# Token scores of the first batch from the state scores, turned by VectorE, in a mixed attention kernel on one core

## The chip, the cores and the metric

The program runs on one core of one Trainium2 chip. Its time is the device time of one execution in microseconds (us), and of several executions the median counts. The engines have queues of their own, in order: TensorE (matmuls), VectorE, ScalarE, GpSimd, and SyncE, which issues the DMAs. A step of one engine waits for steps of another by semaphores.

## The reference

```python
scale = 1.0 / np.sqrt(D)                       # B, H, S, Ns, D = 8, 8, 512, 32, 64
scores = scale * x @ state.T                   # per batch and head: tokens by states
xread = softmax(scores) @ state                # every token reads the state
sread = softmax(scale * state @ x.T) @ x       # every state reads the tokens
x = concat([xread, sread], axis=2)             # 544 tokens of 512 = H * D
logits = x @ w_gate                            # 4 experts, the best 2 of each token
for e in range(4):
    q, k, v = x @ wq[e], x @ wk[e], x @ wv[e]  # 64 wide
    ye = causal_softmax(q @ k.T / 8) @ v @ wo[e]
    out += weight_of_e_for_each_token * ye
```

Both softmaxes of the first part are of the same products x . state: along the states for the tokens, along the tokens for the states.

## The kernel before

Numbers are kept as pairs of 16-bit parts, a high and a low one (`hi_lo` out of PSUM, `split` out of SBUF: one instruction each for the high and the low part), and a product takes three matmuls. A batch goes through four streams. `front` loads x (`xn`), makes the pairs (`xh`), turns them (`xT`), computes the token weights (`eb`, then turned and split into `at`), the state times the weights (`gs`), and from `at` and `gs` the keys `kt`, the values `v`, the gate and the masked queries `qm`. `main` (`probs`, `reads`) does the causal attention in four blocks of 128 tokens. `side` lets the states read the tokens, `tail` does the attention of the 32 state tokens for two batches at once.

The token weights come in one of two ways. Batches from 1 on (`b >= CFG["PA"]`, line 654) call `state_scores`: 24 matmuls of 512 columns give the scores states by tokens in two banks `sa`, from which the state softmax starts (maximum `m2`, exponential `e2`) and which VectorE turns into `eb` (two turns for each half u); the softmax over states follows, VectorE turns the result into `et`, and `split` makes `at`. Batch 0 has 96 small matmuls instead, which give the scores tokens by states in two banks; the softmax reads them there, TensorE turns the weights (4 matmuls for each half, then `hi_lo`), and `side` calls `state_scores` itself.

All steps are numbered as the program makes them, and `run` (line 331) issues them in the written list `ORDER`: number, a dot, and which of a step's possible engines takes it; a third number is a count of fillers, 128-column matmuls on zeros put before the step on TensorE and written to its bank. `SLOTS` gives for each buffer the slot it takes. Both lists come from an offline planner; on the chip each engine follows its own part in order. A warm run of 36 filler matmuls is a step of its own (number 0). The weights of the experts are loaded once in the start-up, in two parts each, into the staging tiles `p32` (384 and 128 KB); `gs` of batch 0 reads them there as they came.

Of the kernel before, what the change touches and what calls it, by code (L numbers as in the profile page):

```python
# [17 lines left out]
           SIDE=32, PX=1, PA=1, LB=1, xn=2, ROUNDS=12, CLIMBS=100, PAT={'PE': 0.15, 'DVE': 0.05},  # L18
# [107 lines left out]
    "mb": "01010101",  # L126
    "p32": "01201222012012010210210201021021021021021",
    "sbm": "01010101",
    "m2": "01010101",
    "s2": "01010101",  # L130
    "kt": "01201020",
    "lg": "010101010101",
# [987 lines left out]
```

## Time and profile before

| | |
|---|---|
| median of three runs | 297.08 us (296.47 to 297.46) |
| the profiled execution's own time | 299.29 us |
| its span in the trace | 297.5 us |
| mean granted TensorE clock | 0.994 of full |
| TensorE matmuls busy | 282.1 us, 95%, 3588 of them |
| VectorE busy | 254.9 us, 86% |
| ScalarE busy | 219.9 us, 74% |
| GpSimd busy | 213.4 us, 72% |

Busy times are shares of the span. Matmuls overlap in their pipeline, so TensorE's busy time includes overlap, and fillers count as busy. Nearly all operations are recorded by one helper (line 347), so they are told apart by the tiles that they write and read, not by their lines.

### The profile page before, as it was taken

What the parts mean: (1) busy time and instruction counts of PE and PEld (TensorE: products, weight loads), DVE (VectorE), ACT (ScalarE), POOL (GpSimd) and SP (SyncE); (2) the same over time, 40 slices, a digit from 0 to 9 for tenths busy, and PEclk for the clock granted to TensorE, in tenths of its full rate; (3) what the DMA queues carried; (4) which work ended last, traced back from release to release, by engine and by line L of the source; (5) the groups of instructions that cost most, each with busy time, mean ns of one, the idle gap of its engine ahead of it and who ended that gap; (6) DMA issues with size and microseconds to landing.
All of it is one profiled execution on the core that took longest, in us unless ns stands there. A gap on an engine that the chain in (4) does not pass through costs nothing. (4 is left out here: it accounts for less than half of the span.)

```text
span 297.5 us, 9631 instructions
## 1 busy us (share of the span) xinstructions
PE 282.1 (95%) x3588; PEld 189.5 (64%) x3588; DVE 254.9 (86%) x783; ACT 219.9 (74%) x677; POOL 213.4 (72%) x293
## 2 busy tenths in 40 slices
PE   8799978898999999999999999999999999999994
PEld 7596565466756565677755586575666667576762
DVE  3877979999999999999999999979998877798640
ACT  4577579889699887977899989646768666647732
POOL 7362787599889797699999995488977942883300
PEclk9979999999999999999999999999999999999999
DMA  7925875998877989999979999988127554385963
GB/s 217 263 47 108 212 121 104 155 236 156 168 158 163 202 176 269 153 173 221 225 152 225 192 155 173 205 184 165 74 65 115 133 97 113 66 156 92 211 197 114
DMA packets 132382, 47.69 MB, mean 160 GB/s; under 512 B 119408, under 2 KB 127856, under 8 KB 132336
## 3 DMA queue, kind: packets, MB, share of 16 engines
q1 hardware_dynamic: 132336, 47.08, 76.9%
q8 instruction: 28, 0.46, 0.7%
q14 instruction: 18, 0.15, 0.2%
HBM read 11.02 MB, written 8.91 MB: 67 GB/s over the span
## 5 line engine op out<-in xcount | busy, mean ns | idle before, releaser
L347 PE MATMUL bank<-kt,qm 128*128 128x128 f16 (+7 forms) x384 | 46.7, 299 | 1.5 <-DVE gs L347 0.7
L347 PE MATMUL bank<-wo_n,z 128*128 128x512 f16 (+1 forms) x198 | 45.8, 373 | 0.1
L347 PE MATMUL bank<-v,pt 128*128 128x192 f16 x480 | 44.8, 246 | 0.9 <-ACT mt L347 0.9
L347 PE MATMUL bank<-at,gs 128*128 128x512 f16 x192 | 45.4, 379 | 0.1
L347 PEld LDWEIGHTS <-pt 128*128 128x128 f16 x480 | 40.4, 98 | 5.8 <-issue 2.3
L347 POOL TENSOR_TENSOR ph<-p,ph 128x256 f16<-128x256 f32 (+3 forms) x22 | 30.8, 1400 | 11.6 <-DVE ph L347 4.3
L347 PEld LDWEIGHTS <-qm 128*128 128x128 f16 (+1 forms) x384 | 23.4, 96 | 22.2 <-issue 8.7
L347 ACT ACTIVATE p<-bank,mx 128x384 f32<-128x384 f32 (+3 forms) x64 | 33.2, 523 | 3.2 <-DVE mx L347 2.3
L347 PEld LDWEIGHTS <-z 128*128 128x128 f16 x198 | 18.5, 98 | 19.5 <-issue 0.8
L347 DVE CUSTOM_DVE_ANT_0 bank<-bank,causal 128x128 f32<-128x128 f32 (+3 forms) x64 | 30.1, 505 | 0.9 <-PE bank L347 0.6
L347 PEld LDWEIGHTS <-gs 128*128 128x128 f16 x192 | 18.1, 99 | 19.6 <-issue 1.3
L347 POOL TENSOR_TENSOR qm<-qf,qm 128x512 f16<-128x512 f32 x21 | 25.9, 1242 | 4.6 <-ACT qm L347 3.9
L347 ACT ACTIVATE o<-bank 128x512 f32<-128x512 f32 (+1 forms) x35 | 19.9, 581 | 7.3 <-PE bank L347 6.7
L347 PE MATMUL bank<-gs,at 128*128 128x260 f16 x192 | 23.6, 273 | 1.1 <-DVE bd L347 0.4
L347 DVE TENSOR_TENSOR qf<-bank,mt 128x512 f32<-128x512 f32 (+1 forms) x32 | 21.3, 683 | 2.4 <-ACT mt L347 2.1
L347 PEld LDWEIGHTS <-at 128*128 128x128 f16 x192 | 18.3, 97 | 6.1 <-issue 1.7
L347 ACT ACTIVATE xh<-xn 128x512 f16<-128x512 f32 (+1 forms) x34 | 19.5, 599 | 3.4 <-DMA xn<-in_x_dram 3.4
L347 POOL TENSOR_TENSOR z<-z 128x128 f32<-128x128 f32 x25 | 12.9, 522 | 10.8 <-DVE z L347 5.4
L345 PE MATMUL bank<-zeros 128*128 128x128 bf16 x236 | 18.1, 247 | 1.4 <-DVE zeros L383 1.0
L347 DVE SCALAR_TENSOR_TENSOR xh<-xn,xh 128x512 f16<-128x512 f32 (+1 forms) x24 | 16.3, 701 | 3.6 <-ACT xh L347 3.2
L345 PEld LDWEIGHTS <-zeros 128*128 128x128 bf16 x236 | 17.1, 114 | 2.6 <-issue 1.6
L347 DVE TENSOR_TENSOR z<-bank,c 128x384 f32<-128x384 f32 x32 | 17.4, 543 | 1.5 <-POOL ph L347 0.9
(193 smaller groups left out, 688.1 us busy)
## 6 DMA issues: line engine op xcount, KB each, us to landing
out_dram<-o SPq DMA_DIRECT2D x33, 256.0 KB, 2.6
xn<-in_x_dram SPq DMA_DIRECT2D x15, 512.0 KB, 4.9
xn<-in_x_dram SPq DMA_DIRECT2D x2, 256.0 KB, 4.1
sn<-in_state_dram SPq DMA_DIRECT2D x16, 32.0 KB, 3.9
p<-in_moe_wo_dram SPq DMA_DIRECT2D x2, 256.0 KB, 5.1
pt<-ph SPq DMA_TRANSPOSE x32, 3.9
z<-zh SPq DMA_TRANSPOSE x29, 2.8
xT<-xh SPq DMA_TRANSPOSE x28, 3.4
```

Source lines behind the costliest of these rows:

```text
L345: self.nc.tensor.matmul(out=to[:, :128], lhsT=self.zeros, rhs=self.zeros, start=True, stop=True, skip_group_check=True)
L347: f(**{k: v.ap() if isinstance(v, View) else v for k, v in kw.items()})
```

## The change

`PA` goes from 1 to 0. Batch 0 then takes the branch of all other batches: `front` calls `state_scores` for it, VectorE turns the scores and the weights, `split` makes `at`, and `side` finds `e2` done. The subtraction of the maximum, which reads SBUF now, may go to GpSimd. `marks["A"]` is not set any more, so the planner is not told to keep the weight splits behind it.

The steps get other numbers: up to 93 they keep theirs; 94 is now the state scores' matmuls; 95 to 100 the state maxima, shifts and exponentials; 101 to 112 the half u=0 (two turns, maximum, subtraction, exponential, sum, plus, reciprocal, product, turn, high part, low part) and 113 to 124 the half u=1; the old 116 to 212 are now 125 to 221, and from the old 220 on all are 2 higher. The list has 2033 steps instead of 2031, and is new throughout, as are the slots. The 130, 125 and 135 of the new list are the matmuls of `gs` with `wk`, `wq` and `wv`; 177 is the first projection. The loads 89 and 90 are of `wk`, 87 and 88 of `wq`, 91 and 92 of `wv`, 318 and 319 of the next batch's x.

```diff
 CFG = dict(ZL=3, GP=1, PT=4, WARM=36, HV=0, BL=1, LEAN0={'DVE': 0.3, 'ACT': 0.0, 'POOL': 0.0}, ZM=4, SM=4, QM=4,
-           SIDE=32, PX=1, PA=1, LB=1, xn=2, ROUNDS=12, CLIMBS=100, PAT={'PE': 0.15, 'DVE': 0.05},
+           SIDE=32, PX=1, PA=0, LB=1, xn=2, ROUNDS=12, CLIMBS=100, PAT={'PE': 0.15, 'DVE': 0.05},
 ORDER = """
...
-5.0 19.0 20.0 21.0 22.0 23.0.41 24.1 4.0 3.0 31.0 1.0 14.0 2.0 8.0 9.0 12.0 26.0 11.0 25.0 32.0 15.0 13.0 27.0 33.0.17 10.0 34.1 35.1 16.0 18.0 17.1
...
+5.0 19.0 20.0 21.0 4.0 3.0 31.0 14.0 12.0 26.0 22.0 2.0 1.0 8.0.48 9.0 32.0 15.0 13.0 27.0 33.0.14 23.0 10.0 24.1 38.0 70.0 45.0 36.0 53.0 41.0 43.0
+81.0 49.0 46.0 39.0 77.0 44.0 54.0 47.0 40.0 51.0 42.0 57.0 82.0 59.0 65.0 72.0 80.0 76.0 71.0 74.0 55.0 75.0 86.0 69.0 58.0 85.0 50.0 66.0 34.1 35.1
+16.0 17.0 18.0 25.0 28.0 29.1 11.0 30.1 94.0.23 113.0 114.0 115.0 0.0 102.0 101.0 103.0 98.0 89.0 202.0 63.0 90.0 205.0 91.0 208.0 7.0 6.0 93.0 214.0
+87.0 92.0 73.0 83.0 37.0 56.0 79.0 61.0 206.1 60.0 116.1 48.0 104.1 88.0 130.0 125.0 135.0 117.0 118.0 119.0 196.0 131.0 105.0 128.0 133.0 95.0 120.0
+121.1 122.0 96.1 126.0 97.0 99.1 123.0 100.0 84.0 198.0 222.0 204.0 207.1 62.0 67.0 68.0 318.0 319.0 106.0 138.0 199.0 326.0 332.0 64.0 124.0 323.0
+320.0 584.0 585.0 590.0.11 329.0 591.0 127.0 107.0 108.0 109.1 327.0 134.0 110.0 129.0 132.0 324.0 328.0 333.1 334.0 111.0 136.0 112.0 211.0 139.0
+592.0 223.0 137.0 325.0 224.0 215.0 330.0 177.0.30 203.0 225.0 178.0 226.0 210.0 78.0 201.1 200.1 197.1 213.1 331.0 227.0 219.0 216.0 588.0 228.0
+229.1 230.0 587.0 586.0 589.0 148.0 321.0 149.0 150.0 151.0 322.0 209.1 174.0 179.0 212.0 144.0 152.0 335.0 175.0 176.0 146.0 147.0 154.0 155.0 336.0
+140.0 145.0 153.0 141.0 337.1 142.0 156.0 220.0 342.0 339.0 157.0 343.0 160.0 158.0 161.0 162.0 354.0 159.0 217.0 338.0 344.0 163.0 340.0 164.0 355.0
...
 SLOTS = {
...
-            st.behind = marks["A"]
+            st.behind = marks.get("A")
```

## Rows read from the trace of the kernel before

**Rows 1.** The table of busy time by stretch. Columns: the stretch, its length, then the busy time and (x instructions) of TensorE's matmuls, its weight loads, VectorE, ScalarE and GpSimd, then the granted clock as a share of full speed, the DMA engines' busy share and GB/s.

```profile
20.00:26.60 6.60, 6.25 (x131) 5.34 (x128) 2.87 (x5) 4.56 (x13) 2.31 (x4) 1.00 0.18 34
26.60:40.00 13.40, 11.91 (x136) 7.21 (x134) 12.08 (x40) 7.54 (x26) 10.67 (x18) 1.00 0.98 190
40.00:100.00 60.00, 55.03 (x727) 36.12 (x727) 57.82 (x182) 53.70 (x171) 50.34 (x50) 1.00 0.78 159
100.00:200.00 100.00, 99.11 (x1216) 64.48 (x1214) 95.77 (x292) 83.28 (x259) 83.60 (x100) 1.00 1.00 193
200.00:280.00 80.00, 79.84 (x983) 52.66 (x981) 66.47 (x218) 53.93 (x176) 53.79 (x65) 1.00 0.56 115
```

**Rows 2.** The time line of TensorE's matmuls in the first 32 us. Columns: start, duration, engine, line, operation, out<-in, shape, how many; in brackets the idle time before them and what ended it. `zeros` are fillers (x36 is the warm run).

```profile
10.00 1.36 PE L347 MATMUL bank<-bd,xT 64*128 64x32 f16 x96 [0.18 <-DVE xT L347]
...
14.39 0.64 PE L347 MATMUL bank<-p,bd 64*32 64x256 f32 x8 [2.04 <-issue]
14.96 5.26 PE L345 MATMUL bank<-zeros 128*128 128x128 bf16 x62
20.06 0.61 PE L347 MATMUL bank<-ident,eb 128*128 128x128 f32 x4
20.50 2.17 PE L347 MATMUL bank<-zeros 128*128 128x128 bf16 x36
...
23.37 0.87 PE L347 MATMUL bank<-xT,bd 64*32 64x512 f16 x23
24.16 0.66 PE L347 MATMUL bank<-ident,eb 128*128 128x128 f32 x4
...
26.62 2.75 PE L347 MATMUL bank<-at,gs 128*128 128x512 f16 x12
```

**Rows 3.** The same view for VectorE.

```profile
8.87 1.43 DVE L347 COPY xT<-bank 128x512 f16<-128x512 f16 x4
11.40 0.69 DVE L347 TENSOR_REDUCE mb<-bank 128x16 f32<-128x512 f32 x1 [1.11 <-PE bank L347]
12.13 0.69 DVE L347 TENSOR_TENSOR eb<-bank,mb 128x512 f32<-128x512 f32 x1
...
14.06 0.68 DVE L347 TENSOR_REDUCE sbm<-eb 128x16 f32<-128x512 f32 x1
...
15.26 0.69 DVE L347 TENSOR_TENSOR eb<-eb,sbm 128x512 f32<-128x512 f32 x1
...
17.33 1.04 DVE L347 SCALAR_TENSOR_TENSOR gs<-bank,gs 128x256 f16<-128x256 f32 x3
...
19.09 0.43 DVE L347 TENSOR_TENSOR wn<-p,wn 128x256 f16<-128x256 f32 x1
...
24.26 1.29 DVE L347 TENSOR_REDUCE m<-bank 128x1 f32<-128x512 f32 x2 [3.73 <-PE bank L347]
25.49 1.29 DVE L347 SCALAR_TENSOR_TENSOR at<-bank,at 128x512 f16<-128x512 f32 x2
...
30.57 0.67 DVE L347 SCALAR_TENSOR_TENSOR kt<-bank,kt 128x512 f16<-128x512 f32 x1
```

**Rows 4.** The table of VectorE's operations by shape from 31 us on: count, total busy us and mean ns of one, idle before.

```profile
L347 DVE STREAM_TRANSPOSE eb<-bank 128x256 f32<-128x256 f32 x28 | 11.5, 429 | 0.2
```

**Rows 5.** The operations on the tile `et` and on `at` from it, in all later batches: minimum, median and maximum ns, first and last start.

```profile
L347 DVE STREAM_TRANSPOSE et<-eb x14: 651/702/723, 48.0 to 227.5; 128x512 f32<-128x512 f32 x14
L347 POOL TENSOR_TENSOR at<-et,at x12: 1152/1156/1604, 50.5 to 231.0; 128x512 f16<-128x512 f32 x12
L347 ACT ACTIVATE at<-et x8: 612/630/642, 48.7 to 169.2; 128x512 f16<-128x512 f32 x8
```

**Rows 6.** The same view for GpSimd's operations on the tile `eb`.

```profile
L347 POOL TENSOR_TENSOR eb<-eb,mb x13: 1039/1047/1049, 37.0 to 212.1; 128x512 f32<-128x512 f32 x13
```

**Rows 7.** The time line of GpSimd in the first 36 us.

```profile
19.33 0.67 POOL L347 TENSOR_SCALAR xn<-xn 128x512 f32<-128x512 f32 x1
20.08 1.47 POOL L347 TENSOR_TENSOR xh<-xn,xh 128x512 f16<-128x512 f32 x1
...
27.67 0.69 POOL L347 TENSOR_SCALAR a<-e,s 128x512 f16<-128x512 f32 x1 [5.28 <-DVE s L347]
```

**Rows 8.** The time line of ScalarE in the first 36 us.

```profile
15.38 0.62 ACT L347 ACTIVATE eb<-eb 128x512 f32<-128x512 f32 x1
...
17.47 1.67 ACT L347 ACTIVATE xh<-xn 128x512 f16<-128x512 f32 x3
```

**Rows 9.** The time line of SyncE's DMA issues in the first 31 us.

```profile
8.77 0.92 SPq L347 DMA_DIRECT2D xn<-in_x_dram  x2
...
10.29 5.37 SPq L347 DMA_DIRECT2D sn<-in_state_dram  x2
...
24.29 5.49 SPq L347 DMA_TRANSPOSE xT<-xh  x4
```

**Rows 10.** The table by stretch again, in single microseconds (columns as in rows 1).

```profile
15.00:16.00 1.00, 1.00 (x17) 1.00 (x14) 0.92 (x2) 0.90 (x3) 0.00 (x0) 0.65 0.29 72
...
18.00:19.00 1.00, 1.00 (x14) 1.00 (x13) 1.00 (x3) 1.00 (x3) 0.89 (x3) 0.64 0.56 73
```

**Rows 11.** DMA issues of the first 40 us by tensor: count, KB each, median us from issue to landing.

```profile
p<-in_moe_wq_dram SPq DMA_DIRECT2D x1, 384.0 KB, 4.4
```

More of the change, by code (lines that the diff above doesn't have):

```diff
@@ L121 @@
     "xh": "0123012301230123",
-    "bank": ("012345670123465270141730524167352416025016374205124617361035715243604152761570214507210541521745214257013217502434106253"
-        "471053264721063425014602534205263402364107642107564320165347016257036425730562405267436041276501256172435642576472156031"
-        "0367425036274356246752370512357024165371023516702365017216573015732416374026132570416235704162357"),
+    "bank": ("012345671320475623017643521764350706352147102745236521603264571072453125043217401234724702147106174362407326412675134026"
+        "157340736251750365170267152076127063146230146532106123457621057423013571204721075325062175462714263072617426371402513720"
+        "146327140672142047615371546023157634102610743621074264731627310523146150327416250367421053647"),
     "bd": "01010101",
     "mb": "01010101",
-    "p32": "01201222012012010210210201021021021021021",
+    "m2": "01010101",
+    "p32": "01202111021021021021021012102102102012012",
     "sbm": "01010101",
-    "m2": "01010101",
     "s2": "01010101",
@@ L140 @@
     "qm": "01010101",
-    "mx": "01230123012301230123012301231023",
+    "mx": "01230123012301230123012301230123",
     "sums": "01010101",
-    "ph": "01010101011010101101010101011010",
+    "ph": "01010101011010101101010101010110",
     "c6": "0101010101010101",
-    "z32": "01201201201012012021201210212012",
-    "zh": "01201201201212012012012021021",
-    "z": "01010101010101010101101010101001",
-    "o": "0123122310231032102310231023103123",
+    "z32": "01201021021201201210210210210210",
+    "zh": "01201201201202102102012012012",
+    "z": "01010101010110101010010010110110",
+    "o": "0123120231023120132013201320132021",
     "tw2": "0101",
+    "twg": "0101",
     "m4": "0101",
-    "twg": "0101",
     "tmt": "0101",
```

168 rows, old and new, of the table ORDER are left out of this document.

## The prediction

> **What bounds the kernel now.** I read the page first (TensorE busy 95% of the span, VectorE 86%), then the table by stretch, then the time lines of TensorE and VectorE up to the first large projection. In the table [rows 1] the reader should see three regimes. Until 26.6 us TensorE's busy time is mostly not work: it holds six runs of fillers and the warm run, whose larger ones stand in [rows 2]. From 26.6 to 100 VectorE is nearly full (12.08 of 13.40 us, then 57.82 of 60) and TensorE loses 1.5 + 5.0 us. From 100 to 280 TensorE is busy 178.95 of 180 us, and nothing is lost. So a gain in the start-up is kept only if it lets VectorE's full stretch begin earlier, and a new order can gain in the first 100 us but only lose behind them.
>
> In the start-up, TensorE's queue [rows 2] shows a jam. Half u=1 of the token weights is final on VectorE at 15.95 us [rows 3]; its turn through TensorE runs at 20.06, behind 62 fillers (5.26 us). The other half's turn waits behind the warm run and the state scores and runs at 24.16. VectorE meanwhile stands still for 3.73 us, because its next instruction reads the state scores [rows 3]. Both halves of `at` are complete at 25.49 + 1.29 = 26.78, and at 26.62 the first projection starts. Nothing of size stands between it and the full stretch.
>
> **The change part by part.** *TensorE.* Removed: 96 token-score matmuls (1.36 us) and two turns (0.61 and 0.66). Moved: the 24 state-score matmuls (0.9 us) from 23.3 to the place of the token scores. Fillers go from 236 to 212, all but 88 (before) and 86 (after) ahead of the first projection. I cost all of it at nothing directly: TensorE waits for `at` in this stretch. Without that cover it would be 1.36 + 1.27 us and some 1.5 us of fillers. The worth is that `at` no longer passes through TensorE's queue.
>
> *VectorE.* Added: four turns of scores out of PSUM (0.429 each alone, 0.38 in a row, so 1.53) [rows 4], two turns of weights (0.70 each, 1.40) [rows 5], one product that GpSimd did (0.69) and one weight part (0.43). Gone to GpSimd: two subtractions (2 x 0.69) and two low parts of `at` (1.29) [rows 3]. Net 4.05 - 2.67 = +1.4 us.
>
> *GpSimd.* Two subtractions at 1.05 [rows 6] and two low parts at 1.16 [rows 5], less one product at 1.05: +3.4 us, hidden in its idle 5.28 us before 27.67 [rows 7].
>
> *When `at` is ready.* The new order needs all of `xT` before the state scores. VectorE does five copies at 0.36 from 8.87 [rows 3], so to 10.65; the scores take 0.9 and the banks are full at about 11.7. VectorE's queue then holds, up to the turn of the second half: four score turns 1.5, two maxima of tokens 1.35 and two of states 1.3, two sums 1.4, four small ones 0.85, two products 1.4, two turns 1.4, and other work put between them (two weight parts, two low parts of `gs`, one 512-column low part of the next batch's x, a small one) 2.3. That is 11.5 us, all from [rows 3 to 5], ending at 23.2. The subtraction and the exponential of each half (1.05 and 0.62) [rows 6, 8] lie beside the other half's turns. Then ScalarE's high part 0.63 and GpSimd's low part 1.16 [rows 5]: 25.0. Two queues can push this: ScalarE must pass four 512-column pieces of the next batch's x (0.56 each) [rows 8], and GpSimd's low part stands behind one piece that it does itself (0.67 + 1.47 us) [rows 7]; either gives 25.2 to 25.5. Against 26.78 that is 1.3 to 1.8 us earlier.
>
> *The same by VectorE's account.* Before, it idles 1.11 + 3.73 = 4.84 us between the copies and the second `kt` low part (which ends at 31.24) [rows 3]. After, I count 1.05 us for the state scores and about 1 us behind ScalarE's pieces of x. 4.84 - 2.05 - 1.4 = 1.4 us gained.
>
> *Queues passed.* On SyncE the weight loads now stand ahead of the next batch's x: that load had to wait for the first `xn` to be read (8.77) [rows 9], so the weights gain its place and lose nothing; x comes at about 16 instead of 13, before ScalarE reaches it near 20.7. The turns of batch 1's x through DMA had to wait until the state scores released `xT` and started at 24.29 [rows 9]; now they wait for VectorE's and GpSimd's low parts alone, and the last is issued near 26.7 instead of 28.5. That, too, is about 1.5 us. On TensorE the new waits are banks: the transposes of the next states take the two banks of state scores, which the exponentials release near 18.2 and 19.8, and the 30 fillers before the first projection take a bank of `gs` released near 20.2. Behind them waits only the first projection, and `at` is later.
>
> *The new order elsewhere.* 2,002 of the steps are in both lists. 85 of them changed engine: VectorE to GpSimd 13, GpSimd to VectorE 16, the rest mostly small ones between VectorE and ScalarE; by the counts and the row durations of such operations this is under 1 us of VectorE in 255. The sequence of TensorE's last twenty steps is the same but for neighbours. I cost it at zero, with both ends from the table: up to 1.5 us better, if a quarter of the 6.5 us lost between 26.6 and 100 goes, and 2 us worse, if the full stretches get 1% of new waits over 200 us.
>
> **The sum.** -1.4 us by either way at the first projection. I take -1.1, because VectorE is full afterwards and part of the earlier start is spent waiting for products of TensorE that start with `at`, not with VectorE. The profiled execution took 299.29 (its span of 297.5 and 1.8 around it), 2.2 above the median of the three timed runs; the sum is a difference, so 298.2 for a like execution and 297.1 - 1.1 = 296.0 for the median.
>
> **The rivals.** *The clock falls and eats the gain (same).* After TensorE's idle 2.04 us at 12.4 to 14.4 [rows 2] the granted clock went to half from about 15.3 to 18.8 [rows 10]: 62 fillers took 85 ns each where 36 at full clock took 60. In the new order TensorE has little from about 16 to 19.8 (it waits for the banks of the state scores) and again for one to three us before `at`. [...] For it: the idle is longer than the one that cost the clock before. Against: 41 fillers stand in between. [...]
>
> *The weight loads block (slower).* Two small loads, the 13th and 14th on SyncE, took 5.37 us to issue at 10.29, right behind x and a weight load [rows 9]. If in the new order it hits the second part of `wq`, the last weight load, it is issued near 15.5 and lands 4.4 later [rows 11], near 20. ScalarE would take the high part of `gs` at 16.4, ahead of the state exponentials and of both high parts of `at`; it would stand for some 4 us and `at` would be ready near 29.3, 2.5 us later than before: 299.6. It decides from a landing later than about 15 us, each us past that costing one. Against it: the 1 MB of x that stood ahead of the two is issued later than `wq` in the new order.
>
> *The new order loses in the full stretches (slower).* Place: 26.6 to 200, where VectorE is busy 96% from 40 on and TensorE 99% from 100 on [rows 1]. One more wait of VectorE per batch of 0.4 us over seven batches is 2.8 us, against the 1.1 gained: 298.8. Nothing in the trace of before speaks for or against it.
>
> *The change does nothing that counts.* If VectorE is the bound up to 60 us and its own work grows, only its idle counts; that is the account above, and if it waits for x 1.4 us longer than I think, the gain is zero. It goes with the clock rival.
>
> **How the numbers follow.** The forecast 0.50, clock or no gain 0.26, weight loads 0.10, order 0.14. Faster or slower by 0.3% (0.9 us) is about what this kernel's measurement can tell. Of the forecast, four fifths are past that (0.40), the rest of it and 0.19 of the no-gain case fall within, and 0.04 of the latter come out faster, from small gains of the order; 0.03 slower. Faster 0.44, same 0.31, slower 0.25. The forecast's own range is 294.2 to 297.0 (-3 us, if the order gains 1.5 too, to nothing). The whole range goes to 298.8, which takes in the clock case and the order's loss and leaves the weight loads out.
>
> **What would show it.** Right: no idle of VectorE above 1.5 us between 11.7 and 25; `at` complete at 25 to 25.5; the first projection within 0.5 us of that; batch 1's first DMA turn before 23. Wrong: a granted clock below 1 in the 4 us after the first projection's start; ScalarE idle before a `gs` high part near 16; TensorE idle between 100 and 200 above 2 us; GpSimd late with the subtractions at 13 us, because its constants are not done.

## The result, and the profile after

The changed kernel takes 298.26 us (median of 20 executions, 297.75 to 299.43), the kernel before, run beside it on the same chip, 296.79 (20 executions, 295.30 to 299.67): ratio 1.0053, 95% interval [1.0031, 1.0075], so 1.5 us slower where 1.1 us less was forecast. Single executions of either kernel and of the later runs that took 465 to 978 us are left out of the ratios and the spans; the medians that count one move by at most 0.22 us. The profiled execution took 298.13, its span is 296.3, its mean granted clock 0.994.

The table by stretch, columns as in [rows 1]:

```profile
20.00:26.60 6.60, 5.31 (x49) 4.36 (x49) 6.37 (x18) 4.32 (x10) 5.14 (x5) 0.77 0.44 83
26.60:40.00 13.40, 12.05 (x181) 8.02 (x181) 12.75 (x39) 8.50 (x28) 10.94 (x17) 1.00 0.81 182
40.00:100.00 60.00, 55.21 (x722) 36.16 (x716) 58.33 (x179) 52.44 (x168) 50.00 (x50) 1.00 0.86 162
100.00:200.00 100.00, 99.51 (x1205) 64.78 (x1200) 95.13 (x295) 83.52 (x260) 87.41 (x103) 1.00 1.00 193
200.00:280.00 80.00, 80.00 (x977) 52.47 (x976) 69.13 (x223) 53.28 (x166) 47.76 (x57) 1.00 0.57 116
```

VectorE is busy 6.37 of 6.60 us in the first row, where it was 2.87: its standstill is gone. Behind 100 us TensorE loses next to nothing (99.51 of 100, 80.00 of 80). TensorE's time line, as in [rows 2]:

```profile
13.48 0.66 PE L347 MATMUL bank<-p,bd 64*32 64x256 f32 x16
15.18 1.10 PE L347 MATMUL bank<-p,bd 64*32 64x256 f32 x32 [1.03 <-DMA p<-in_moe_wq_dram]
...
18.14 0.33 PE L347 MATMUL bank<-ident,sn 128*128 128x128 f32 x1 [1.83 <-ACT e L347]
19.92 1.33 PE L345 MATMUL bank<-zeros 128*128 128x128 bf16 x11 [1.45 <-ACT e L347]
...
21.26 2.68 PE L345 MATMUL bank<-zeros 128*128 128x128 bf16 x30
23.82 0.38 PE L347 MATMUL bank<-at,gs 128*128 128x512 f16 x1
25.49 1.24 PE L347 MATMUL bank<-at,gs 128*128 128x512 f16 x5 [1.29 <-POOL at L347]
...
30.82 0.84 PE L347 MATMUL bank<-xT,bd 64*32 64x512 f16 x24 [0.80 <-DMA xT<-xh]
```

The last row but one is what the start-up is about: five of the first six projection matmuls start at 25.49, released by GpSimd's low part of `at`. Before, the projection started at 26.62 in the trace. What stands ahead of it, on VectorE, GpSimd and SyncE (as in [rows 3, 7, 9]):

```profile
11.50 0.78 DVE L347 STREAM_TRANSPOSE eb<-bank 128x256 f32<-128x256 f32 x2 [0.92 <-PE bank L347]
...
22.41 0.70 DVE L347 STREAM_TRANSPOSE et<-eb 128x512 f32<-128x512 f32 x1
```

```profile
13.08 1.05 POOL L347 TENSOR_TENSOR eb<-eb,mb 128x512 f32<-128x512 f32 x1 [0.15 <-DVE mb L347]
14.56 1.05 POOL L347 TENSOR_TENSOR eb<-eb,mb 128x512 f32<-128x512 f32 x1 [0.15 <-DVE mb L347]
...
22.72 1.16 POOL L347 TENSOR_TENSOR xh<-xn,xh 128x512 f16<-128x512 f32 x1
23.85 1.59 POOL L347 TENSOR_TENSOR at<-et,at 128x512 f16<-128x512 f32 x1
```

```profile
11.34 0.51 SPq L347 DMA_DIRECT2D p<-in_moe_wq_dram  x1
...
13.04 1.19 SPq L347 DMA_DIRECT2D sn<-in_state_dram  x2
22.22 5.67 SPq L347 DMA_TRANSPOSE xT<-xh  x4
```

And the granted clock by stretch, columns as in [rows 1]:

```profile
19.00:20.00 1.00, 0.08 (x2) 0.08 (x2) 1.00 (x3) 1.00 (x4) 0.65 (x1) 0.80 0.00 0
20.00:23.00 3.00, 3.00 (x29) 2.93 (x29) 2.93 (x7) 2.90 (x7) 1.64 (x3) 0.50 0.00 0
23.00:24.00 1.00, 1.00 (x17) 0.91 (x16) 1.00 (x4) 0.86 (x3) 1.00 (x2) 1.00 0.49 97
```

After TensorE's idle 1.83 and 1.45 us the granted clock was 0.50 for the fillers from 20 to 23, and 1.00 from 23 to 24, ahead of the projection.

So the trace of after does nearly all that the prediction said, and its span is 1.2 us shorter than the traced one of before. Yet it is slower in the median. The next part finds out why.

### The profile page after: what moved, and what is told of

The parts are those of the page before. It is cut to its first block, busy times and chain, and to the rows that moved or that the text cites. A ratio compares the mean times of both kernels' runs of the same rounds, so it can differ in the third digit from the quotient of the medians.

```text
span 296.3 us, 9386 instructions
## 1 busy us (share of the span) xinstructions
PE 278.6 (94%) x3460; PEld 186.3 (63%) x3460; DVE 260.6 (88%) x797; ACT 220.1 (74%) x675; POOL 214.4 (72%) x288
## 4 chain that ended last, share of the span: by engine, by line
PE 54%; DVE 8%; ACT 5%; issue 1%; ACTq 0%
PE bank L347 54%; ACT p L347 1%; DVE bank L347 1%; DVE gs L347 1%; DVE xh L347 1%; ACT xh L347 1%; ACT e L347 1%; DVE sbm L347 1%; DVE a L347 1%; DVE mb L347 1%; ACT kt L347 1%; DVE z L347 1%; DVE tmx L347 0%; ACT eb L347 0%; DVE ph L347 0%
## 5 line engine op out<-in xcount | busy, mean ns | idle before, releaser
L347 PE MATMUL bank<-kt,qm 128*128 128x384 f16 (+7 forms) x384 | 46.6, 299 | 0.7 <-ACT p L347 0.2
L347 ACT ACTIVATE p<-bank,mx 128x128 f32<-128x128 f32 (+3 forms) x64 | 33.1, 522 | 2.7 <-DVE mx L347 2.2
L347 POOL TENSOR_TENSOR qm<-qf,qm 128x512 f16<-128x512 f32 x21 | 24.9, 1199 | 3.9 <-ACT qm L347 3.4
L347 POOL TENSOR_TENSOR zh<-z,zh 128x256 f16<-128x256 f32 x24 | 16.3, 683 | 10.2 <-ACT zh L347 3.9
L347 DVE SCALAR_TENSOR_TENSOR xh<-xn,xh 128x512 f16<-128x512 f32 (+1 forms) x23 | 17.0, 755 | 4.3 <-ACT xh L347 4.3
L345 PE MATMUL bank<-zeros 128*128 128x128 bf16 x212 | 16.9, 251 | 2.9 <-ACT e L347 1.9
L347 POOL TENSOR_TENSOR at<-et,at 128x512 f16<-128x512 f32 x13 | 16.0, 1234 | 4.0 <-ACT at L347 3.4
```

The costliest lines, as they stand in the source:

```text
L345: self.nc.tensor.matmul(out=to[:, :128], lhsT=self.zeros, rhs=self.zeros, start=True, stop=True, skip_group_check=True)
L347: f(**{k: v.ap() if isinstance(v, View) else v for k, v in kw.items()})
```

## The experiments

Theory S: the start-up decides, and the traced execution of before had an unusual start-up. Theory R: the new order loses behind it. Shown times are medians; each ratio is to before on the same chip (296.73 to 297.56 in its medians). The ratios are not the quotients of the medians and differ from them by up to 0.4%; where the two say different things, both are given.

**Before again, two mixed lists, fewer fillers.** The hybrids join the start of one list (215 and 212 entries) to the sequence of the other; the tiles' buffers are given out anew. The first lines of their edits (h1 against after, h2 against before), and the edit of b_fill14:

```diff
-140.0 145.0 153.0 141.0 337.1 142.0 156.0 220.0 342.0 339.0 157.0 343.0 160.0 158.0 161.0 162.0 354.0 159.0 217.0 338.0 344.0 163.0 340.0 164.0 355.0
+140.0 153.0 339.0 355.0 142.0 141.0 145.0 156.0 337.1 342.0 340.0 160.0 157.0 161.0 343.0 162.0 220.0 354.0 158.0 338.0 341.0 217.0 344.0 159.0 356.0
...
```

```diff
-337.0 353.0 133.0 132.0 136.0 147.0 335.1 340.0 338.0 151.0 148.0 152.0 341.0 153.0 211.0 352.0 149.0 336.0 339.0 208.0 342.0 150.0 354.0 154.0 430.0
+334.0 136.0 132.0 335.1 133.0 147.0 211.0 340.0 337.0 148.0 341.0 151.0 149.0 152.0 153.0 352.0 150.0 208.0 336.0 342.0 154.0 338.0 155.0 353.0 156.0
...
```

```diff
-113.0.62
+113.0.14
```

> The kernel before, unchanged, for a second trace and the spread of its executions. Its twenty times reach from 295.3 to 299.7 us, the changed kernel's only from 297.8 to 299.4, and the profiled execution of before (299.3) was one of the longest. If the change lost against a start-up that is usually better than the one in that trace (theory S, start-up), a usual execution (295.5 to 297 us) starts the first projection clearly before 26.6 us, at 24 to 25.5, and the rest, from that start to the end of TensorE's work, takes 266 us as before. If the start-up is always like the traced one and the new order loses behind it (theory R, rest), the first projection stands at 26.6 us again and a shorter execution is shorter behind it.

> The changed start-up (the new order's first 215 entries, to batch 0's last value matmul), then all other steps in the sequence of the order before; bank slots given out anew. Theory S: the loss is in the start-up, so this kernel is as slow as the changed one, ratio 1.004 to 1.008 to before. Theory R: the start-up gains about 1 us and the old sequence behind it keeps it: ratio 0.995 to 0.998.

> The reverse: the start-up of before (its first 212 entries, batch 0 with its own token scores and TensorE turns), then the new order's sequence for all the rest. Theory S: equal to before, ratio 0.998 to 1.002. Theory R: the loss shows here, and by more than in the changed kernel, which gained in the start-up: ratio 1.006 to 1.010.

> Before, with 14 instead of 62 fillers ahead of the turn of the half u=1 on TensorE. If the fillers held up the start-up in the usual execution too, the turn runs at 16 to 17 us instead of 20.1, VectorE's 3.7 us of idle shrink, and the first projection starts up to 2 us earlier: ratio 0.993 to 0.997. If it is held by the weights' landing near 20 us or by VectorE anyway, the ratio is 0.999 to 1.001; if the missing fillers let the granted clock fall at the first projection, 1.002 to 1.006.

Measured: b_again 296.95, ratio 0.9997 [0.9961, 1.0033] (its trace is too unlike the timed executions to show a usual start-up); h1 300.74, 1.0106 [1.0061, 1.015]; h2 305.82, 1.0276 [1.0226, 1.0325]; b_fill14 299.98, 1.0086 [1.0051, 1.0121]. Both hybrids are slower than either parent, so they do not tell S and R apart; that a list fitted to one start loses with another is a reading of this, not shown. But h2 has the start-up of before, step for step, and its trace shows another course of it: the wait inside the matmuls on `p` is 0.90 us instead of 2.04 [rows 2], the 62 fillers take 3.64 us instead of 5.26, and the first projection starts at 24.27, not 26.62. Behind it h2 needs 278.2 us, with one wait of 3.76 us for ScalarE's `e` ahead of 38.3. In b_fill14 the projection started at 22.55, yet the time was longer (276.0 us behind it, outside all that was expected): TensorE waited 2.03 us for the DMA turn of `a` up to 37.5, and from 38 to 41 us its granted clock was 0.50, after TensorE had been busy 0.51 of 2 us. So an early start alone is not enough:

```profile
36.00:38.00 2.00, 0.51 (x17) 0.51 (x17) 1.99 (x6) 1.35 (x5) 0.89 (x2) 0.98 0.90 259
38.00:41.00 3.00, 3.00 (x61) 2.91 (x57) 0.97 (x3) 0.49 (x2) 2.82 (x4) 0.50 0.03 10
```

**A second trace of before, and an earlier `at` in the changed kernel.** b_again2 has no edit. The three others edit after:

```diff
-132.0 324.0 328.0 333.1 334.0 111.0 136.0 112.0 211.0 139.0
+132.0 111.0 112.1 324.0 328.0 333.1 334.0 136.0 211.0 139.0
```

```diff
-132.0 324.0 328.0 333.1 334.0 111.0 136.0 112.0 211.0 139.0
-592.0 223.0 137.0 325.0 224.0 215.0 330.0 177.0.30
+132.0 324.0 330.0 328.0 333.1 334.0 111.0 136.0 112.0 211.0
+139.0 592.0 223.0 137.0 325.0 224.0 215.0 177.0.30
```

```diff
-132.0 324.0 328.0 333.1 334.0 111.0 136.0 112.0 211.0 139.0
-592.0 223.0 137.0 325.0 224.0 215.0 330.0 177.0.30
+132.0 111.0 112.1 324.0 328.0 333.1 334.0 136.0 211.0 139.0
+330.0 592.0 223.0 137.0 325.0 224.0 215.0 177.0.30
```

> The kernel before, unchanged, for a second trace of it. Theory S (the difference lies in the start-up, and the traced execution of before had an unusual one): the trace shows a start-up in which the eight matmuls on p wait about 0.9 us instead of 2.04, the 62 fillers take about 3.6 us instead of 5.26, the first projection starts at 24.0 to 24.6 instead of 26.62, the granted clock is 1.00 from 15 us on, and behind the first projection it takes the 270.5 to 271 us that both traced kernels took (26.62 to 297.5 and 25.49 to 296.3), so its span is 294.5 to 295.5. Theory R (the new order loses behind the start-up): the first projection stands near 26.6 here too, or the time behind it is more than 1 us shorter than the 270.8 of the changed kernel.

> The changed kernel with one step changed: the low part of at for half u=0 is made by VectorE, behind its second gs low part, instead of by GpSimd behind a piece of the next batch's x. at is then complete at about 24.5 instead of 25.44 and the first projection starts 0.9 us earlier. VectorE's low parts of the next batch's x come 0.7 us later, so the state scores of batch 1 (30.82 in the changed kernel, behind a wait of 0.80 for xT) come at about 31.5. Theory S, if the first projection alone decides: 0.9 us under the changed kernel, ratio to before about 1.002. Theory S2, if the batch-1 scores (their xT) decide: 0 to 0.7 us slower than the changed kernel, ratio 1.005 to 1.008. Theory R (the loss sits behind the start-up): no change against the changed kernel, ratio 1.005.

> The changed kernel with one step moved: VectorE's last low part of the next batch's x stands right behind the one before it (at 24.4 instead of 25.42), ahead of two gs low parts and four small ones. at and the first projection stay at 25.4; the last DMA turn of batch 1's x is issued 1 us earlier, and the state scores of batch 1 come at about 30.0 instead of 30.82. Theory S (first projection alone): no change, ratio 1.005. Theory S2 (the batch-1 scores): up to 0.8 us under the changed kernel, ratio 1.0025. Theory R: no change.

> Both edits: the low part of at for half u=0 on VectorE, and the last low part of the next batch's x moved up behind the first gs low part of 260 columns. First projection at about 24.5, batch-1 state scores at about 30.5. Theory S and S2 both: 0.5 to 0.9 us under the changed kernel, ratio to before 1.002 to 1.003, as each us of the start is worth a us. Theory R: no change, ratio 1.005. If instead a list fitted for one start-up loses with any other (as the two hybrids suggest), all three edits are slower than the changed kernel by 1 us or more.

Measured: b_again2 299.77 (one execution); a_lo 299.43, 1.0088 [1.0056, 1.0119]; a_xh 299.04, 1.0069 [1.0043, 1.0094]; a_lo_xh 299.32, 1.0078 [1.0047, 1.0109]. The trace of b_again2 repeats the unusual start to within 0.02 us; TensorE's time line:

```profile
11.30 1.07 PE L347 MATMUL bank<-p,bd 64*32 64x256 f32 x24
14.39 0.64 PE L347 MATMUL bank<-p,bd 64*32 64x256 f32 x8 [2.02 <-issue]
14.96 5.26 PE L345 MATMUL bank<-zeros 128*128 128x128 bf16 x62
...
26.61 2.75 PE L347 MATMUL bank<-at,gs 128*128 128x512 f16 x12
```

It stops behind 24 of 32 matmuls for 2.02 us, waiting for nothing that the profile shows, and most of the 62 fillers behind the stop run at half clock (0.64 in the slice from 15 to 16, 0.65 in that from 18 to 19). So the usual start of before was still not seen here: S not settled. Of the three edits of after two made `at` earlier (a_lo: six matmuls at 24.49; a_lo_xh: five at 24.90), and all three lost. What they have in common lies further on: ahead of the 30 fillers that run at 36.2 us in after TensorE waits 2.47 us (a_lo), 1.88 (a_xh) and 1.78 (a_lo_xh) for ScalarE's `e`, in after 0.43. TensorE's rows of after and of a_lo:

```profile
36.22 1.83 PE L345 MATMUL bank<-zeros 128*128 128x128 bf16 x30 [0.43 <-ACT e L347]
```

```profile
38.00 2.76 PE L345 MATMUL bank<-zeros 128*128 128x128 bf16 x30 [2.47 <-ACT e L347]
```

ScalarE starts the first `e` there at 37.19, 36.54 and 36.52 instead of 35.40. VectorE runs late from its low part of `a` on (27.65, 28.09 and 28.06 instead of 26.95), and in a_lo ScalarE, ahead of `e`, waits another 0.98 us for the output weights `wo`, whose load SyncE issues behind the first DMA turn of `a`. In a_lo the state scores of batch 1 came at 30.56, no later than in after (30.82), and the granted clock fell from 36 to 42 us:

```profile
36.00:42.00 6.00, 4.00 (x57) 3.99 (x57) 5.19 (x21) 4.54 (x13) 4.66 (x7) 0.72 0.82 148
```

In a_xh the instruction that I moved up fell beside GpSimd's low part of `at`; VectorE's row and GpSimd's:

```profile
23.77 2.31 DVE L347 SCALAR_TENSOR_TENSOR xh<-xn,xh 128x512 f16<-128x512 f32 x2
```

```profile
23.95 1.59 POOL L347 TENSOR_TENSOR at<-et,at 128x512 f16<-128x512 f32 x1
```

Two such low parts took 0.69 + 0.68 us in a_lo_xh, here 2.31: the second ended only after GpSimd's, and VectorE's next steps came a us late. In a_lo_xh TensorE waited 0.79 us for a low part of `gs` behind the first six matmuls. An earlier `at` alone is not kept in this list; what stands behind it on VectorE came later.

**The exchange rate of the start, VectorE beside GpSimd, a shifted stream.** The edits: b_late, a_late, a_xh813, b_shift:

```diff
-168.0.7
+168.0.27
```

```diff
-177.0.30
+177.0.74
```

```diff
-617.0 618.1 638.0 630.1 813.0 296.0
+617.0 618.1 813.0 638.0 630.1 296.0
```

```diff
-23.0.41
+23.0.45
```

> The kernel before with 27 instead of 7 fillers ahead of its first projection: 20 x 60 ns = 1.2 us at full clock, so that it starts at 25.5 where it usually starts at 24.3, as in the changed kernel (25.49). Theory S (the changed kernel is slower because its first projection starts 1.2 us later than that of a usual execution of before, us for us): 296.8 + 1.2 = 298.0, ratio 1.004, the same as the changed kernel. Theory R (the new order loses behind the start-up and the start-up is worth nothing): 296.8 to 297.2, ratio at most 1.0015. Any trace of it that has TensorE's wait of 2 us before 14.4 starts its projection at 27.8 instead.

> The changed kernel with 74 instead of 30 fillers ahead of its first projection (44 x 60 ns = 2.6 us): they end near 26.4, so that five of the six first projection matmuls start at about 26.5 instead of 25.49. Theory S: 1.0 us slower than the changed kernel, ratio to before 1.0085. If VectorE's queue sets the time there and not TensorE's: less than 0.4 us slower, ratio 1.005 to 1.0065.

> The changed kernel with one instruction of VectorE moved up by one place: the low part of batch 3's x that took 1.57 us at 73.87, beside GpSimd's product of 1.16 at 73.73, now stands ahead of the gs low part, at 73.2, where GpSimd waits. Theory C (VectorE's instructions that read and write SBUF alone stand still while GpSimd works on SBUF; the new order puts more of them side by side, 10.3 us of excess in VectorE's instructions against 5.2 before, and VectorE sets the time up to 100 us): this instruction takes 0.7 us, the state scores of batch 3 start 0.5 to 0.9 us before 87.61, and the time is 0.3 to 0.9 us lower, ratio 1.002 to 1.004. Without C: the instruction takes 1.57 us there too, or nothing changes behind it, ratio 1.005.

> The kernel before with four more fillers in its first run, at 2 us, where TensorE waits for x anyway: the time of before, ratio 1.000, for a trace of a usual execution. Theory S: if its trace has no TensorE wait of 2 us before 14.4, the 62 fillers take about 3.6 us, the first projection starts at 24.0 to 24.6, the granted clock is 1.00 behind 15 us and the span is 294.5 to 295.5, which is 270.5 to 271.2 behind the first projection. Theory C adds: VectorE's excess in instructions stretched beside GpSimd is about 5.2 us in it, as in the two traces of before.

Measured: b_late 299.08, 1.0062 [1.0027, 1.0097]; a_late 301.56, 1.0115 [1.0066, 1.0163]; a_xh813 298.93, 1.0045 [1.0013, 1.0078]; b_shift 295.93, 0.9948 [0.9914, 0.9982]. b_shift, for which 1.000 and a start at 24.0 to 24.6 were expected, shows the start-up of before without the stop:

```profile
11.30 1.36 PE L347 MATMUL bank<-p,bd 64*32 64x256 f32 x32
12.60 3.63 PE L345 MATMUL bank<-zeros 128*128 128x128 bf16 x62
16.07 0.61 PE L347 MATMUL bank<-ident,eb 128*128 128x128 f32 x4
...
20.17 0.66 PE L347 MATMUL bank<-ident,eb 128*128 128x128 f32 x4
...
22.63 2.75 PE L347 MATMUL bank<-at,gs 128*128 128x512 f16 x12
```

The rows down to the projection are the same steps as in b_again2, and the projection starts 4.0 us earlier: 2.0 of the wait, 1.6 of the fillers, which take 59 ns each instead of 85, and 0.3 because the interrupted matmuls took 1.07 + 0.64 us instead of 1.36. And here the span follows us for us: 293.7 - 22.63 = 271.1 us behind the first projection, where the traces of before have 270.9 and 271.4 and that of after 296.3 - 25.49 = 270.8. Delaying the start costs at least the delay: b_late starts at 26.09 (behind a stop of 1.49) and ends 271.7 behind it; 1.2 us of fillers cost 1.8 us by the ratio. a_late starts at 27.17, 1.7 us later than after, and is 1.8 us slower by the ratios, 3.2 by the medians of its chip; its span is 272.6 behind the start, with 2.7 us of TensorE's waits for DMA turns between 100 and 280 us. This is what S says, with more than S in a_late.

a_xh813 was for a third theory, C: that VectorE's instructions lose where GpSimd works on SBUF beside them. The row of after and that of a_xh813 for the same instruction, with GpSimd's beside it in after:

```profile
73.87 1.57 DVE L347 SCALAR_TENSOR_TENSOR xh<-xn,xh 128x512 f16<-128x512 f32 x1
```

```profile
73.73 1.16 POOL L347 TENSOR_TENSOR qm<-qf,qm 128x512 f16<-128x512 f32 x1 [0.86 <-ACT qm L347]
```

```profile
73.66 0.68 DVE L347 SCALAR_TENSOR_TENSOR xh<-xn,xh 128x512 f16<-128x512 f32 x1
```

The 0.9 us of that instruction are saved, and nothing comes of it: from batch 2's state scores to batch 3's it took 30.28 us, in after 29.90, and against after the time is 0.2 us less by the ratios and 0.5 more by the medians, inside the intervals. The stretched instruction is real, but did not set the time there. C falls for one of its two largest pieces; the others were not tried.

**The same shifts for both kernels.** In before `23.0.41` becomes 37, 45 or 53, in after `8.0.48` becomes 44, 52 or 60: fillers in the first run, at about 2 us, where TensorE waits for x anyway. b_plus4 is b_shift once more; a second start of it was not seen.

> The kernel before with four more fillers in its first run, once more. If its gain is real: ratio 0.993 to 0.998 again, spans of 292.5 to 295 and none with a clock of 0.994. Theory S: the traced execution again takes 271 us (270.5 to 271.7) from its first projection to the end of the span, wherever the projection starts. If the gain was chance: ratio 0.998 to 1.002 with some executions at 0.994.

> The kernel before with twelve more fillers in its first run, at 2 us, beside waiting. If the wait of TensorE hangs on where the instruction stands in its stream: the stop moves eight matmuls further forward, out of the second group of p matmuls, and the time is that of the copy with four more, ratio 0.993 to 0.998. If it hangs on the moment alone: ratio 0.997 to 1.002, spans as wide as those of before. Either way the trace takes 271 us behind the first projection.

> The kernel before with four fillers fewer in its first run. If the wait hangs on the place in the stream: the stop moves four matmuls back, into the last four of the sixteen, and is reached later by 0.15 us; ratio 0.997 to 1.003, a wait of up to 2 us in the trace after about 28 of 32 matmuls. If it hangs on the moment alone: the same ratio, but the stop stays behind 24 matmuls.

> The changed kernel with four more fillers in its first run. Theory S: nothing changes, ratio to before 1.004 to 1.007, because at comes out of VectorE's and GpSimd's queues at about 25.4 whatever TensorE waits for ahead of it; the trace takes 271 us behind the five matmuls that wait for at. If TensorE's stop cost the changed kernel time too: up to 1 us faster, ratio 1.002.

> The changed kernel with four fillers fewer in its first run. Theory S: its first projection stays at 25.4 to 25.6 and is later than the mean start of before, so it is slower than before at this shift too (before at this shift: 1.0025): ratio 1.004 to 1.012. If the difference between the two kernels is only one of shifts: ratio under 1.0025, as likely below before as above it.

> The changed kernel with twelve more fillers in its first run. Theory S: first projection at 25.4 to 25.6, ratio 1.004 to 1.012 (before at this shift: 1.0005). If the difference is only one of shifts: ratio under 1.0025.

| fillers | before: median, ratio | after: median, ratio |
|---|---|---|
| -4 | 298.10, 1.0025 [0.9988, 1.0063] | 298.31, 1.0046 [1.0018, 1.0075] |
| 0 | 296.79, 1 | 298.26, 1.0053 [1.0031, 1.0075] |
| +4 | 295.88, 0.9945 [0.992, 0.9971] | 300.63, 1.0128 [1.0091, 1.0165] |
| +12 | 297.55, 1.0005 [0.9976, 1.0034] | 302.68, 1.0197 [1.0147, 1.0246] |

The gain of four fillers is real: before with `23.0.45` beats both kernels, and none of its 21 executions was above a span of 294.8. The changed kernel is above before at each shift (at -4 by less than the intervals can tell), though the rows come from several chips. But I had expected a_plus4 to change nothing, and it cost 0.75%, 2.2 us. Its first projection starts at 25.57, that of a_plus12 at 25.51, as in after; they lose behind it, 273.0 and 274.6 us instead of 270.8. (a_minus4 starts at 26.00, later than expected, with 271.2 behind it.) TensorE's waits from 100 to 280 us, in after and in a_plus12 (what was waited for: us in total, times, longest):

```profile
PE bank L347 <- DVE bank L347: 0.2, 1, 0.2
PE bank L347 <- DVE z L347: 0.2, 1, 0.2
```

```profile
PE bank L347 <- DMA z<-zh: 1.8, 2, 1.4
PE bank L347 <- DMA a2t<-a: 1.7, 2, 1.0
...
```

The 3.5 us of these two kinds of wait, where after has none, are nearly all of the 3.8 us that a_plus12 takes longer behind its start; in a_plus4 it is 2.1 us of waits for `z` and 2.2 us. Why a few fillers at 2 us make turns late 100 to 270 us further on stays open. Before has it too, where 271 was expected: b_minus4 needed 272.3 us behind a start at 25.43, and b_plus12 273.5 behind one at 23.12. No single wait accounts for it: the wait of 1.9 us for `a2t` in b_plus12 has its like in b_again2 (1.8), which needed 271.4. And the stop is not all that moves a start: in b_minus4 it is 0.58 us, but the 96 token-score matmuls start at 11.89 instead of 10.00. So S fits the difference at the shift that was timed, and not that at +4 and +12.

## Why the prediction was wrong

**Right, by its own steps.** No idle of VectorE above 1.5 us from 11.7 to 25 (0.92 at 10.6, then none); `at` complete at 23.85 + 1.59 = 25.44 (25.2 to 25.5 was said); the first projection at 25.49; batch 1's first DMA turn issued at 22.22 (before 23); GpSimd's subtractions 0.15 us behind VectorE; the weights issued by 11.85, and though TensorE waited 1.03 us for the second part of `wq`, to 15.18, nothing that `at` needs came late (in a_plus12 that wait lasts to 15.96, and the projection starts at 25.51), so that rival is out; the half clock (0.50 from 20 to 23) taken by fillers and over before the projection, so that rival is out too. What such a stretch would have cost in the projection no run shows; in before it cost the 62 fillers 1.6 us. The new order costs nothing behind the start at the shift that was timed: 270.8 us against 270.9 and 271.4. That the -1.1 us came out between the two traced executions (299.29 and 298.13, so -1.16) is in part luck: the start moved by 1.13 us, not 1.4, and nothing was lost behind it, where 0.3 was allowed for; and four more fillers would have made the piece behind 273.0.

**The step that failed is the base of the sum.** The prediction took 1.1 us off a trace whose first projection starts at 26.62 and wrote: "the sum is a difference, so 298.2 for a like execution and 297.1 - 1.1 = 296.0 for the median". The 298.2 is the measured time (298.26): start 25.49, 270.9 behind it, 1.8 around. The 296.0 is not, since the 2.2 us by which the profiled execution stood above the timed ones lay, by all that the runs show, in the very piece that the change takes away: the stop of 2.04 us, the half clock behind it (62 fillers in 5.26 us instead of 3.64) and so the late turns of the token weights through TensorE. The text had read both rows [rows 2, 10] and taken them for the jam of every execution.

Of the 127 executions of before with a clock on record, 110 had a mean clock of 0.997 to 1.000 and spans of 292.4 to 296.9 (median 295.05); 17 had 0.989 to 0.994, and spans of 297.0 to 299.6. Both traces of before are of the second kind (0.994; 297.5 and 298.0). Their clock is that of the half clock in the start-up alone: 3.4 us at half in a span of 297.5 make a mean of 0.994, by estimate. So the 110 did not have that half clock, which cost 1.6 us of fillers. An estimate of the usual start from these numbers: 295.05 - 271.1 = 24.0 us, beside 22.63 and 24.27 in b_shift and h2, which have that start-up and a short stop or none. The estimate is a middle value: with 271.1 us behind it the shortest span, 292.4, would start at 21.3, earlier than any trace, so the time behind the start varies as well. The changed kernel has its start at 25.49 and spans of 296.0 to 297.6 in all 20 executions: 1.5 us later by the starts, 1.5 slower by the medians. So the change made the start-up steady, at a place later than the usual one. Not shown is a trace of an unchanged before in a usual execution; its start is inferred. Nor is it shown why both traces fell on the rarer kind.

**The rivals.** None of them is what happened. "The change does nothing that counts" came nearest, but by VectorE's idle; the time was lost to the old start-up being better than its trace. "The new order loses in the full stretches", with one more wait of 0.4 us per batch, is not in the trace of after; at two other shifts the loss is there, from DMA turns, in a size that no part of the sum had.

**Terms that were mis-sized without effect.** VectorE's busy time grew by 5.7 us (254.9 to 260.6), not 1.4, GpSimd's by 1.0 (213.4 to 214.4), not 3.4. Much of VectorE's growth is instructions that stood beside GpSimd's, of which the new order has more; the shape table of the low parts of x from 26 us on, before and after (count, busy us, mean ns, idle before):

```profile
L347 DVE SCALAR_TENSOR_TENSOR xh<-xn,xh 128x512 f16<-128x512 f32 x16 | 11.4, 730 | 0.2
```

```profile
L347 DVE SCALAR_TENSOR_TENSOR xh<-xn,xh 128x512 f16<-128x512 f32 x15 | 12.8, 856 | 0.0
```

Over the whole time line 17 instructions of VectorE took over 0.25 us more than the median of their operation and shape, together 8.5 us; before it was 11 with 4.4 us. (The sums of 10.3 and 5.2 us in an expectation above go by another measure of what is usual.) Each of the 28 ran beside an instruction of GpSimd, and none of them reads or writes a bank. That GpSimd's +3.4 us are "hidden in its idle 5.28 us" left out what its work does to VectorE. Two sums of the prediction are off without effect too: 81 fillers of before, not 88, stand behind the place of the first projection, and its cases add up to 0.29 for the same time and 0.27 for slower, not 0.31 and 0.25.

## What to carry to other kernels

When the profiled execution is longer than the timed ones, look first for the piece that makes it so: a wait that the profile puts down to nothing (here 2.04 us), a stretch at half clock (here 3.4 us). Compare the trace's mean clock with that of the timed executions (here 0.994 against 0.997 to 1.000). If the change takes that piece away, add up the new time from its start (here 25.5 + 271 + 1.8) instead of taking a difference from a trace that the usual execution does not resemble. And a gain of one us in a kernel that moves by one or two when a few idle instructions are added should be timed at several such shifts before it is believed.

## What the runs showed of the hardware

**TensorE stopped in the start-up, waiting for nothing that the profile shows.** The stop in the start-up was 2.04, 2.02, 1.49, 0.90 and 0.58 us in five traces of the old start-up, about 0.1 us in two (b_fill14, b_plus12) and none in b_shift, always in the matmuls on `p`, with the DMA engines at 100% (the share column of 11 to 13 us is 1.01 and 1.00 in before; without a stop, in b_shift, it is 0.98 and 1.08). It moves with the stream: behind 24 of 32 matmuls in before, behind 28 with four fillers fewer, behind 12 with twelve more. So it does not hang on the data of one matmul. What TensorE stood for in it no run shows, and the lack of any stop in b_shift is not explained.

**An instruction of VectorE took longer beside one of GpSimd.** A low part of x (two inputs and the output in SBUF) took 0.68 us in a_xh813, where GpSimd's product began 0.58 us behind it, and 1.57 in after, where GpSimd's 1.16 us product had begun 0.14 us earlier: it ended at 75.44, 0.55 behind the product's end at 74.89. It counts as busy. What held it no run shows.
